# Chunked attention, Fourier mix and MLP: batch 0's first row half unfolded, half sine tables, a second scores buffer, loads in another order

## The chip, the core and the metric

One core of one Trainium2 chip runs the kernel. The metric is the device time of one execution in microseconds, the median of the runs. TensorE is called PE here, VectorE DVE, ScalarE ACT, GpSimd POOL, SyncE SP. PE multiplies into PSUM banks; DVE and ACT read them; POOL works on SBUF only, and the DMA transfers that it starts go out on a queue of its own, as those of SP do on theirs.

## What is computed

```python
# q, k, v: (4, 8, 768, 64); mem_k, mem_v: (4, 8, 8, 64)
for c in range(24):                       # chunks of 32 queries
    k_full = concat(mem_k, k[c_start - 16 : c_end + 8])      # clipped to 0..768
    v_full = concat(mem_v, v[c_start - 16 : c_end + 8])
    out[c] = softmax(q[c] @ k_full.T / 8) @ v_full
x = out as (4, 768, 512)
u = x + real(fft(fft(x, axis=1), axis=2))
un = (u - mean(u)) / sqrt(var(u) + 1e-6)
y = u + relu(un @ w_ch1) @ w_ch2          # w_ch1 (512, 2048), w_ch2 (2048, 512)
```

The real part of the two transforms needs cosine and sine tables over the 768 rows (cosS, sinS) and over the 512 columns (cosD, sinD).

## The kernel before

The four batches go through the same three stages: attention, Fourier mix, MLP. A small planner (class Plan, lines 37 to 174) orders every step: each step has an engine, a cost, what it waits for, the slots that it takes and gives, and a rank. `order` walks through time, puts on each idle engine the ready step of lowest rank, and the instructions are then emitted in that order; on the chip each engine runs its list strictly. Where PE has no ready step between two given events, the planner emits a filler, a multiplication of zeros (`e_fill`, line 899).

**Attention** (line 941) works on pairs of heads, four pairs per batch, in the order 0, 2, 1, 3; n counts them, so n = 0 to 3 is batch 0 and n = 4 the first of batch 1. Per pair, Q and K are loaded by POOL's queue (L349), V by SP's queue in pieces of 256 bytes a row (L358, L362, L367). PE turns Q and K (L377, tiles trq and trk), ACT copies Q (L395), DVE or ACT copies K into kTb (L420) beside the memory keys (L408). Then, for each of two halves g, PE multiplies scores (L433, tile sc, two banks), ACT takes the exponentials (L441, two instructions of 1.05 us together), PE multiplies the values (L457, tile xa for g = 0 and xo for g = 1), and DVE divides by the sums (L467, L468) into the rows of xsb. The one sc tile serves all pairs and both halves. Q and K stage through three buffers each, V through four (va). Rows 0 to 31 of each va are filled with zeros once by ACT (L331), its edges by POOL or DVE, and POOL puts in the ones at the edges (L322, L324, L327) before that pair's V is loaded. POOL also makes the masks (L301 to L307) that the exponentials use. A copy on POOL from the last V tile of batch 0 (L956, "gate") holds back the loads of batch 1.

**Tables.** DVE works out the angles (L920 to L928), ACT takes the sines (L1027 to L1031) of all 2 x 3 x 193 entries for the rows and 2 x 256 for the columns, DVE makes negated copies (L1035, L1038) and sets the first row (L1040, L1041). ACT then loads the table of the exponential (L1048).

**Fourier mix of batch 0** (`first_fourier`, line 1071). The columns 0 to 127 and 256 to 383 come from the pairs n = 0 and 1, the others from n = 2 and 3. For each row half g (three tiles of 128 rows), DVE adds and subtracts the columns (L599), folds them with their mirror image (L610, two steps), ACT rounds to a 16-bit high part (L651), DVE takes the low part (L655), and PE multiplies both parts with the tables (L688: four sums ps, 12 multiplications each and per half). One extra row is handled apart (L661 to L664 on POOL, L669 and L675 on PE). The second half is folded by L616 and L635. Then ACT and DVE split the sums again (L541, L546, L554), PE multiplies over the columns (L699), DVE adds to x (L705) and takes mean and variance (L713), and PE turns the result (L730) for the MLP.

**MLP.** W1 and W2 are loaded by POOL's queue (L1062, L1067), W1 once the second half's first fold is placed, W2 after pair 6's loads (n = 6). Layer 1 is L775, ReLU L784, layer 2 L793 or, for later batches, L842 with sums of weights (L817). PE works on the MLP of one batch while attention and Fourier mix of the next run. PSUM has two banks under the name acc, two under mlp, and tiles tr, sc (two banks) and xa.

Of the kernel before, what the change touches and what calls it, by code (L numbers as in the profile page):

```python
# [10 lines left out]
FP32 = mybir.dt.float32  # L11
# [10 lines left out]
MEM0 = 32  # L22
# [14 lines left out]
class Plan:  # L37
# [6 lines left out]
    WARM = 18.0  # L44
# [47 lines left out]
    def order(self):  # L92
# [9 lines left out]
        while any(waiting.values()):  # L102
# [5 lines left out]
            for e, ts_ in waiting.items():  # L108
# [49 lines left out]
                else:  # L158
                    if e == "PE" and self.filling and self.filling[0]["at"] is not None \
                            and self.filling[1]["at"] is None:  # L160
                        cost = self.FILL * (2.0 if now < self.WARM else 1.0)
                        idle[e] = now + cost
                        placed.append(dict(engine="PE", cost=cost, emit=self.fill, at=now,
                                           done=now + cost))
                        moved = True
# [12 lines left out]
def kernel(  # L178
# [25 lines left out]
    NK = 193  # L204
    HD = DM // 2
# [11 lines left out]

    bank_of, bank_free = {}, {"acc": [0, 1], "mlp": [0, 1]}

    def bank(tag, shape, dtype, name):  # L220
        i = bank_free[tag].pop(0)
        t = fps.tile(shape, dtype, tag=f"{tag}{i}", bufs=1, name=name)
        bank_of[name].append((t, tag, i)) if name in bank_of else bank_of.update({name: [(t, tag, i)]})
        return t
# [12 lines left out]
    ks = [spool.tile([P, 2, RB * D], BF16, name=f"ks{i}") for i in range(NS)]  # L237
    NV = 4
# [25 lines left out]
    tri = fpool.tile([P, 3, 2, HD], FP32, tag="hT", bufs=1, name="tri")  # L264
    kk, yD, rD = tri[:, 0], tri[:, 1], tri[:, 2]
    yS = fpool.tile([P, 3, 2, NK], FP32, tag="fold", bufs=2, name="yS")
    rS = fpool.tile([P, 3, 2, NK], FP32, tag="fold", bufs=2, name="rS")
    sv = cpool.tile([P, 3], FP32)
    svS = cpool.tile([P, 3], FP32)
    svD = cpool.tile([P, 1], FP32)  # L270
    zero = cpool.tile([P, 1], FP32)
# [10 lines left out]
    odd = wpool.tile([P, 2, 3, NK], FP16)  # L282
    cosD = wpool.tile([P, 2, HD], FP16)
# [10 lines left out]
    def e_iota():  # L294
        nc.gpsimd.iota(kk, pattern=[[1, 2], [2, HD]], base=0, channel_multiplier=0,
# [4 lines left out]
    def e_masks():  # L300
# [6 lines left out]
        nc.gpsimd.memset(mbias[MEM0:MEM0 + NMEM, 1:2], 0.0)  # L307

# [20 lines left out]
    def e_low_rows(i):  # L329
        low = va[i][0:MEM0].rearrange("p h t c -> p (h t c)")  # L330
        nc.scalar.copy(low, zero[0:MEM0].to_broadcast([MEM0, 2 * NT * 66]))  # L331
# [8 lines left out]
    def e_load_qk(n, i):  # L340
        b, pr = seq[n]
        src, dst = ((q, qs), (k, ks))[i]
        if b >= TURNED:
            for hh in range(2):
                nc.gpsimd.dma_start(
                    strided(dst[n % NS], hh * D, [[2 * D, NST], [1, D]]),
                    src[b, 2 * pr + hh].rearrange("(a p) d -> p a d", p=P))
            return
        nc.gpsimd.dma_start(dst[n % NS][0:QP],  # L349
# [30 lines left out]
    def e_flip_q(n):  # L380
        qT_of[n] = qT = apool.tile([P, S], BF16, tag="qT", bufs=2, name="qT")
        nc.sync.dma_start_transpose(qT.rearrange("p (a s) -> p a s", s=P),
                                    qs[n % NS].rearrange("p h c -> p (h c)")[:, 0:S])

    def e_flip_k(n):
        nc.sync.dma_start_transpose(kU[n % NKU][:, KR:KR + S].rearrange("p (a s) -> p a s", s=P),
                                    ks[n % NS].rearrange("p h c -> p (h c)")[:, 0:S])

    def e_turn_q(n):
        tr_of[n] = trq = aps.tile([P, S], BF16, tag="tr", bufs=1, name="trq")  # L390
        turn(trq, qs[n % NS][0:QP], ident_b[0:QP, 0:QP])

    def e_qT(n):
        qT_of[n] = qT = apool.tile([P, S], BF16, tag="qT", bufs=2, name="qT")
        nc.scalar.copy(qT.rearrange("p (a j) -> p a j", j=RB),  # L395
                       tr_of.pop(n).rearrange("p (j a) -> p a j", j=RB))

    def e_turn_k(n):
        if n < HP:
            trk = bank("acc", [P, RB * KP], BF16, "trk")  # L400
        else:
            trk = aps.tile([P, RB * KP], BF16, tag="tr", bufs=1, name="trk")
        tr_of[n, 1] = trk
        turn(trk, ks[n % NS][0:KP], turn_b)

    def e_mkT(n):
        b, pr = seq[n]
        (nc.scalar.copy if n == HP else nc.vector.tensor_copy)(  # L408
# [17 lines left out]
    def e_scores(n, g):  # L426
        qT, kT = qT_of[n], kTb[n % NKT]
        sc_of[n, g] = sc = aps.tile([P, 2, 8, 64], FP32, tag="sc", bufs=1, name="sc")
# [50 lines left out]
    mid32 = cpool.tile([P, NST, 1], FP32)  # L479
# [63 lines left out]
    def e_rest(b, par, ab):  # L543
# [4 lines left out]
        let_go(ps)  # L548
# [44 lines left out]
    def g_zy(par, g):  # L593
        if g == 0:
            if par == 0:
                both = fpool.tile([P, 2, NST, P], FP32, tag="dn", bufs=1, name="zy0")
                zy_of[0, 0], zy_of[0, 1] = both[:, 0], both[:, 1]
# [4 lines left out]
    def g_ff(par, ab, g, last):  # L602
        if (ab, g, last) == (0, 0, 0):
            ff_of[0, par] = fpool.tile([P, 2, NST, P], FP32, tag="fold", bufs=2, name="ff0")
        xb, sl = xs[0][:, 3 * g:3 * g + 3], slice(3 * g, 3 * g + 3)
        zy, ff = zy_of[0, par][:, sl], ff_of[0, par][:, ab, sl]
        plus = ab == par
        if last:
            plus = plus == (par == 0)
        nc.vector.tensor_tensor(ff[:, :, 1:P], (ff if last else zy)[:, :, 1:P],  # L610
                                rev_ap(xb, 2 * P - 1 + HD * last, P - 1, [[DM, 3]]),
                                ALU.add if plus else ALU.subtract)
# [6 lines left out]
    def g_col(par, ab, g):  # L619
        zy = zy_of[0, par]  # L620
        ff = ff_of[0, par][:, ab, 3 * g:3 * g + 3]
        if ab == 0:
            nc.scalar.copy(ff[:, :, 0], zy[:, 3 * g:3 * g + 3, 0])
        elif par == 0:
            nc.scalar.copy(ff[:, :, 0], zero[:, 0:1].to_broadcast([P, 3]))
        elif g == 1:
            nc.scalar.copy(ff[:, :, 0], zy[:, 0:3, 0])
        else:
            xb = xs[0][:, 0:3]
            nc.gpsimd.tensor_tensor(ff[:, :, 0], xb[:, :, P], xb[:, :, HD + P], ALU.subtract)  # L630
# [18 lines left out]
    def g_hi(par, ab, g):  # L649
        sl = slice(3 * g, 3 * g + 3)  # L650
        nc.scalar.copy(g_hl(par, 0)[:, ab, sl], ff_of[0, par][:, ab, sl])  # L651

    def g_lo(par, ab, g):
        sl = slice(3 * g, 3 * g + 3)
        nc.vector.tensor_tensor(g_hl(par, 1)[:, ab, sl], ff_of[0, par][:, ab, sl],  # L655
                                g_hl(par, 0)[:, ab, sl], ALU.subtract)

    def g_mid(g):
# [743 lines left out]
```

## Time and profile before

| | |
|---|---|
| time, median of 3 | 282.46 us (281.37 to 285.58) |
| the profiled execution | 282.55 us, span 280.7 us |
| PE busy | 264.3 us (94%) |
| DVE busy | 193.5 us (69%) |
| ACT busy | 155.2 us (55%) |
| POOL busy | 64.3 us (23%) |
| the chain that ended last | PE 84%, DMA 7%, DVE 4%, SP's queue 3% |

Busy time of PE holds the fillers too, and matmuls are pipelined, so it is not work alone. All times in the views count from the first instruction of the span. A group of matmuls with tile names shows what it multiplies: trq is the turned Q, trk the turned K, sc scores, xa and xo values, ps sums over rows, pm sums over columns, ph and pc the two layers, idle the fillers.

Loads and their landings in the first 70 us, from the trace (issue, then landing):

| load | issue | landing |
|---|---|---|
| Q, K of n = 0 | 1.54, 3.06 | 6.03, 9.75 |
| Q, K of n = 1 | 4.75, 5.40 | 12.02, 13.53 |
| Q, K of n = 2 | 8.00, 8.64 | 15.07, 16.01 |
| Q, K of n = 3 | 16.54, 17.18 | 21.43, 23.64 |
| Q, K of n = 4 | 27.98, 28.60 | 32.17, 33.16 |
| W1, four pieces | 34.05 to 35.71 | 42.41 to 50.51 |
| W2, four pieces | 37.51 to 45.31 | 56.44 to 66.25 |
| Q, K of n = 7 | 48.27, 51.07 | 67.51, 68.75 |

V of n = 0 to 3 is issued from 1.36, 6.47, 15.17 and 18.58 us on.

### The profile page before, as it was taken

Reading aid. Unit: us, or ns where it says so; the run is one execution under the profiler, and the core shown is the slowest. Engines: PE = TensorE matmul, PEld = TensorE weight load, DVE = VectorE, ACT = ScalarE, POOL = GpSimd, SP = SyncE. Lnnn points to the kernel's source line nnn. Section 1 sums busy time; section 2 is a strip of 40 time slices with the busy share of each in tenths; the row PEclk is TensorE's granted clock in tenths of the full one; section 3 lists DMA queues with packets and bytes.
Section 4 is the critical chain, followed back from the end, with each engine's and each line's share of the span. In section 5 each row is a group of like instructions: output and inputs, shape, how many; then the busy total and the mean of one; then the engine's idle time right before and its main releaser. Section 6 shows DMA issues by size and latency. Waiting matters only on the chain.

```text
span 280.7 us, 7981 instructions
## 1 busy us (share of the span) xinstructions
PE 264.3 (94%) x3325; PEld 207.4 (74%) x3325; DVE 193.5 (69%) x424; ACT 155.2 (55%) x262; POOL 64.3 (23%) x127
## 2 busy tenths in 40 slices
PE   0589999999999999998999999999999999999995
PEld 0466698788756579766668766858988888888884
DVE  7968978970218979899688776599869825353444
ACT  6887667579665757734745665525526270605150
POOL 8840853240111038306200230101004100000000
PEclk9999999999999999999999999999999999999999
DMA  6989999999899969999999734497101507103152
GB/s 102 199 143 174 162 206 204 196 198 201 162 190 236 214 103 220 177 142 144 235 191 209 177 74 109 108 207 167 48 37 58 131 21 168 40 37 77 50 103 76
DMA packets 116116, 39.98 MB, mean 142 GB/s; under 512 B 104560, under 2 KB 111472, under 8 KB 116080
## 3 DMA queue, kind: packets, MB, share of 16 engines
q1 hardware_dynamic: 93888, 23.54, 46.9%
q0 software_dynamic: 21472, 15.21, 34.0%
q10 hardware_dynamic: 720, 0.72, 0.7%
q8 instruction: 26, 0.43, 0.7%
q14 instruction: 10, 0.08, 0.1%
HBM read 37.36 MB, written 13.37 MB: 181 GB/s over the span
## 4 chain that ended last, share of the span: by engine, by line
PE 84%; DMA 7%; DVE 4%; SPq 3%; issue 1%; POOL 0%; POOLq 0%
PE ph L775 31%; PE pc L793 15%; PE pc L842 13%; DMA va<-in_v_dram 6%; PE ps L529 6%; PE xa L457 4%; PE pm L699 4%; PE ps L688 3%; PE xo L457 3%; PE sc L433 2%; SPq L358 2%; DMA qs<-in_q_dram 1%; PE trk L377 1%; PE trq L377 1%; DVE xsb L705 1%; PE pm L580 1%
## 5 line engine op out<-in xcount | busy, mean ns | idle before, releaser
L775 PE MATMUL ph<-unT,w_sb 128*128 128x256 f16 x768 | 90.3, 273 | 0.8 <-DVE xsb L800 0.8
L784 ACT ACTIVATE hT<-ph 128x512 f16<-128x512 f32 x96 | 56.9, 598 | 54.3 <-PE pc L842 30.2
L775 PEld LDWEIGHTS <-w_sb 128*128 128x128 f16 x768 | 73.2, 98 | 11.1 <-issue 1.7
L793 PE MATMUL pc<-w_sb,hT 128*128 128x512 f16 x192 | 44.8, 380 | 0.0
L441 ACT ACTIVATE e<-sc,mbias 128x384 f32<-128x384 f32 x64 | 33.6, 576 | 19.0 <-PE sc L433 19.0
L793 PEld LDWEIGHTS <-hT 128*128 128x128 f16 x192 | 17.7, 98 | 19.0 <-issue 0.2
L847 DVE TENSOR_TENSOR xsb<-pc,xsb 128x256 f32<-128x256 f32 x43 | 18.0, 421 | 12.4 <-PE pc L842 10.6
L842 PEld LDWEIGHTS <-hT 128*128 128x128 f16 x240 | 23.3, 98 | 4.2 <-DVE hT L830 1.0
L842 PE MATMUL pc<-w_sb,hT 128*128 128x256 f16 x192 | 24.1, 272 | 0.5 <-DVE hT L830 0.5
L541 ACT CAST up<-ps 128x386 f16<-128x386 f32 x16 | 9.7, 605 | 17.6 <-PE ps L529 17.0
L830 DVE TENSOR_TENSOR S<-hT 128x768 f16<-128x768 f16 (+1 forms) x12 | 5.1, 422 | 18.5 <-ACT hT L784 17.9
L800 DVE SCALAR_TENSOR_TENSOR xsb<-pc,rstd,xsb 128x512 f32<-128x512 f32 x12 | 9.0, 750 | 12.2 <-PE pc L793 12.1
L713 DVE BATCH_NORM_STATS2 st<-xsb 128x6 f32<-128x512 f32 x24 | 16.6, 690 | 0.6
L705 DVE TENSOR_TENSOR xsb<-pm,xsb 128x512 f32<-128x512 f32 x15 | 10.2, 678 | 7.1 <-PE pm L699 6.9
L457 PEld LDWEIGHTS xa<-va,e 128*64 128x64 f32 x384 | 12.5, 137 | 3.2 <-issue 2.0
L457 PE MATMUL xa<-va,e 128*64 128x65 f32 x384 | 14.7, 226 | 0.0
L433 PEld LDWEIGHTS <-kTb 64*128 64x128 bf16 x384 | 7.8, 96 | 9.0 <-issue 8.1
L457 PE MATMUL xo<-va,e 128*64 128x65 f32 x384 | 14.1, 223 | 0.0
L546 DVE TENSOR_TENSOR up<-ps,up 128x386 f16<-128x386 f32 x16 | 9.6, 602 | 6.1 <-ACT up L541 6.1
L395 ACT COPY qT<-trq 128x768 bf16<-128x768 bf16 x12 | 9.5, 793 | 6.4 <-PE trq L377 6.4
L572 POOL DMA_DIRECT2D xr<-x_back x3 | 2.3, 770 | 46.7 <-DMA x_back<-x_rows 46.7
L519 DVE TENSOR_TENSOR lo<-ff,hi 128x768 f16<-128x768 f32 x12 | 11.3, 954 | 2.4 <-ACT hi L514 2.4
(168 smaller groups left out, 455.3 us busy)
## 6 DMA issues: line engine op xcount, KB each, us to landing
va<-in_v_dram SPq DMA_DIRECT2D x32, 220.0 KB
w_sb<-in_moe_w_ch_dram POOLq DMA_DIRECT2D x8, 512.0 KB, 16.9
out_dram<-xsb SPq DMA_DIRECT2D x12, 256.0 KB
qs<-in_q_dram POOLq DMA_DIRECT2D x12, 192.0 KB, 6.5
ks<-in_k_dram POOLq DMA_DIRECT2D x12, 192.0 KB, 7.0
x_rows<-xsb POOLq DMA_DIRECT2D x3, 768.0 KB, 4.6
xr<-x_back POOLq DMA_DIRECT2D x3, 768.0 KB, 5.0
out_rows<-xsb SPq DMA_DIRECT2D x9, 256.0 KB
```

Of the source, the lines that this page charges most:

```text
L433: nc.tensor.matmul(sc[:, hh, t6, :], kT[r0:r0 + 64, t, :], qT[r0:r0 + 64, ts(t, 64)], start=True, stop=True, tile_position=(r0, 0))
L441: nc.scalar.activation(e1[:, :, :, ts(half, 32)], sc[:, :, 0:6, ts(half, 32)], AFT.Exp, bias=mbias[:, half:half + 1], scale=1.0 / math.sqr ...
L457: nc.tensor.matmul(xa[64 * half:64 * half + 64, st, hh, 0:65], e1[:, hh, t6, :], v1[:, hh, 6 * g + t6, 0:65], start=True, stop=True)
L519: nc.vector.tensor_tensor(lo[:, ab].rearrange(fl), ff_of[b, par][:, ab].rearrange(fl), hi[:, ab].rearrange(fl), ALU.subtract)
L529: nc.tensor.matmul(out_[:, sp, :], part[:, ab, sp * 3 + st, c0:c1], tab[:, sp, st, :], start=(st == 0 and i == 0), stop=(st == 2 and i == 1))
L705: nc.vector.tensor_tensor(uv, pm_of[b, kt], uv, ALU.add)
L713: nc.vector.bn_stats(st6, xs[b][:, kt, :])
L775: nc.tensor.matmul(ph[:, k, :], w1_sb[:, dt, ts(HH * k + i, P)], unT_of[b, j][:, dt, :], start=(dt == 0), stop=(dt == NDT - 1))
L784: nc.scalar.activation(hT_of[b, j][:, :, i, :], ph, AFT.Relu, bias=0.0, scale=1.0 if b in EVEN else -1.0)
L793: nc.tensor.matmul(pc_of[b, j, r], hT_of[b, j][:, k, i, ts(r, P)], w2_sb[:, HH * k + i, :], start=(i + k == 0), stop=(i + k == HH))
L842: nc.tensor.matmul(pc_of[key], a[:, i, :], w[:, i, :], start=(i == 0 and new), stop=(i == HH - 1), skip_group_check=not new)
L847: nc.vector.tensor_tensor(u, pc, u, ALU.add)
```

## The change

**First row half of batch 0, unfolded.** Instead of folding columns with their mirror before the multiplication, the forward columns (of n = 0 and 1) and the mirrored ones (of n = 2 and 3) are multiplied apart and summed in PSUM; where the fold subtracted, the mirrored product uses a negated table (neg for sp = 0, odd for sp = 1). The sums ps of par 0 lie in the sc tile, those of par 1 in acc.

```diff
+    def g_back(par):
+        nc.vector.tensor_tensor(ff_of[0, par][:, 0, 0:3, 1:P],
+                                rev_ap(xb, 2 * P - 1, P - 1, [[DM, 3]]),
+                                rev_ap(xb, 2 * P - 1 + HD, P - 1, [[DM, 3]]),
+                                ALU.add if par == 0 else ALU.subtract)
+    def g_rows0(par, ab, back):
...
+        for sp in range(2):
+            tab = ((neg, odd)[sp][:, ab] if back and ab != par else (cosS, sinS)[ab][:, sp])
+            for st in range(3):
+                for i in range(2):
+                    nc.tensor.matmul(ps[:, sp, :], g_hl(par, i)[:, back, st, :], tab[:, st, :],
+                                     start=(not back and sp + st + i == 0), stop=False)
...
+                        take=() if back else ("acc",) if par else ("sc",) if ab == 0 else ())
+                    if (par, ab, back) == (1, 0, 1):
+                        t_e2 = add("POOL", 0.4, g_edge2, [t_e1, t_ra[1, 0]], rank=20.2)
```

Column 0 of the mirrored half is set to zero by POOL (`g_edge0`), and for par 1 it takes the middle column, made by POOL before DVE's `g_w` overwrites its input (`g_edge1`) and put in place between the third and the fourth mirrored product (`g_edge2`). The extra row is now multiplied once, after its halves are added and subtracted on POOL (`g_mid`, five small operations; `g_row`, 12 multiplications, no zeroing multiplication).

**Tables by half.** Angles and sines are worked out for 97 of 193 row entries and 129 of 256 column entries; DVE mirrors the rest with a sign (`e_back_S`, `e_back_D`, four instructions, and six on one column in `e_signs`); POOL writes the last column (`e_tails`), makes neg (`e_negatives0`, two instructions of 579 elements) and takes over nsinD and the row memsets.

```diff
-            nc.scalar.activation(sinS[:, par], rS[:, :, par], AFT.Sin, bias=0.0, scale=scS)
+            nc.scalar.activation(sinS[:, :, :, 0:NH], rS.rearrange(order), AFT.Sin, bias=0.0, scale=scS)
+        nc.vector.tensor_scalar(tab[:, :, :, NH:NK - 1],
+                                strided(tab, NH - 2, [[3 * NK - 1, 2], [NK, 3], [-1, NH - 2]]),
+                                sign[:, 1 - i:2 - i], None, ALU.mult)
+    def e_negatives0(i):
+        nc.gpsimd.tensor_scalar(neg[:, i], (cosS, sinS)[i][:, 0], -1.0, None, ALU.mult)
-        nc.vector.tensor_scalar(nsinD, sinD, -1.0, None, ALU.mult)
+        nc.gpsimd.tensor_scalar(nsinD, sinD, -1.0, None, ALU.mult)
```

**Scores in two places.** The two acc banks become views of one tile, accs. In batch 0 the second half's scores (g = 1) go there, the first half's to sc; the turned K of batch 0 goes to mlp instead of acc.

```diff
+    accs = fps.tile([P, 2, 512], FP32, tag="acc", bufs=1, name="accs")
+        sc_of[n, g] = sc = (accs.rearrange("p h (t q) -> p h t q", q=64) if n < HP and g == 1 else
+                            aps.tile([P, 2, 8, 64], FP32, tag="sc", bufs=1, name="sc"))
```

**Loads and small work.** Pair 3 of batch 0 has a stage of its own (last_qk, in the space of w2t), and its loads are issued right behind pair 2's (rank 10.2). The gate reads the first head of pair 3's last V tile instead of the second. W2 is loaded after pair 7's Q and K instead of after pair 6's. Low rows of va 2 and 3 become memsets on POOL, the memory-key copies of batch 0 (`e_mkT`) move from DVE to POOL. The K copies of n = 5, 6, 7 move from ACT to DVE. The turns of a pair in batch 0 get ranks ahead of the scores of the pair before. The weight sums on DVE (`e_w2t`) are placed behind batch 2's statistics.

```diff
-        t_low[i] = add("ACT", 1.45, lambda i=i: e_low_rows(i), [t_zero, e_],
-                       rank=(0, 1, 2, 3)[i])
+        t_low[i] = add("ACT" if i < 2 else "POOL", 1.45 if i < 2 else 1.7, lambda i=i: e_low_rows(i), [t_zero, e_],
+                       rank=(0, 1, 17.3, 17.4)[i])
+                      rank={0: -4 + i, 1: -1.2 + 0.1 * i, 2: 10 + 0.1 * i, 3: 10.2 + 0.1 * i}.get(n)) for i in range(2)]
-            if b == 1 and i in (1, 2):
+            if b == 1 and i in (1, 3):
```

**Fillers.** They now start with the first one at the head of the program (before: with the first scores) and end when the first half product's input is ready (before: when the first folded one is). Each filler takes any free one of the slots mlp, tr and xa for its own length; the planner counts PE as slow until 6 us instead of 18.

```diff
-    WARM = 18.0
+    WARM = 6.0
+                        tag = next((x for x in ("mlp", "tr", "xa") if self.free[x] > 0), None)
-                        plan.filling = (t_sc[0, 0], add("PE", 0.0, lambda: let_go(fill_of[0]), [lo],
-                                                        give=("mlp",)))
+        plan.filling = (t_fill, add("PE", 0.0, lambda: None, [half[0, 0]]))
```

POOL's list in batch 0, by rank: first loads and edge ones, kTb zeros and memory keys, loads of pairs 2 and 3, pad memset of K, tails, masks (16), edges of va 2 and 3 (17), further pads, edge ones of va 2 and 3 (17.1), low rows (17.3, 17.4), neg (17.5, 17.6), edge zeros (18, 19), column-table rows (19.5), kU zeros (20), then the gate and batch 1's loads, with the edge column and the extra row (20.1 to 20.3) ahead of them where ready.

## The prediction

> **What bounds the kernel now.** I read the page's strip of 40 slices first, because it tells where TensorE (PE) is not full.
>
> ```profile
> PE   0589999999999999998999999999999999999995
> DMA  6989999999899969999999734497101507103152
> ```
>
> PE is full from the fourth slice (21 us) to the last: what is not full is the start. The change works there, so the next view is busy time by stage. Columns: stretch, length, then busy us (instructions) of PE, its weight loads, DVE, ACT, POOL; granted clock, DMA share, GB/s.
>
> ```profile
> 0.00:9.00 9.00, 0.77 (x4) 0.26 (x6) 7.48 (x28) 5.52 (x6) 7.75 (x22) 1.00 0.76 123
> 9.00:22.00 13.00, 10.54 (x239) 8.00 (x239) 10.40 (x29) 11.89 (x20) 7.72 (x24) 1.00 1.05 170
> 22.00:33.20 11.20, 10.70 (x226) 7.42 (x224) 9.80 (x24) 7.27 (x18) 4.45 (x10) 1.00 1.00 160
> 33.20:57.10 23.90, 23.25 (x391) 20.34 (x389) 20.79 (x49) 14.68 (x28) 9.80 (x16) 1.00 1.16 201
> ```
>
> The first multiplication of the MLP (L775) starts at 57.1. Up to there PE is busy 45.26 us and idle 11.84. Part of the busy time is filler (L902, multiplications of zeros), as the same stretches restricted to tile idle show (PE busy first):
>
> ```profile
> 0.00:9.00 9.00, 0.50 (x1) 1.00 0.76 123
> 9.00:22.00 13.00, 2.02 (x6) 1.00 1.05 170
> 22.00:33.20 11.20, 4.59 (x23) 1.00 1.00 160
> ```
>
> With 0.14 after 33.2 that is 7.24 us, so work is 45.26 - 7.24 = 38.0 of the 57.1 us. After 57.1 the waits of PE sum to 0.8 + 0.5 us and a tail of some 3. The end therefore moves by what the start of the MLP moves, if nothing behind it runs dry.
>
> The timeline says why the start is slow (start, length, what, idle before it):
>
> ```profile
> 8.95 0.85 PE L377 MATMUL trq<-ident_b,qs 96*64 96x96 bf16 x16
> 9.79 0.88 PE L377 MATMUL trk<-turn_b,ks 100*64 100x100 bf16 x16
> 16.55 1.05 ACT L441 ACTIVATE e<-sc,mbias 128x384 f32<-128x384 f32 x2 [1.08 <-PE sc L433]
> 17.49 1.50 ACT L331 COPY va<-zero 32x1584 f32<-32x1584 f32 x1
> 18.29 0.52 PE L377 MATMUL trk<-turn_b,ks 100*64 100x100 bf16 x16
> 27.44 0.47 POOL L956 COPY gate<-va 1x1 f32<-1x1 f32 x1 [9.63 <-DMA va<-in_v_dram]
> 33.43 1.17 PE L675 MATMUL ps<-cosS,mid 128*1 128x193 f16 x12
> ```
>
> The eight pairs of exponentials of batch 0 run from 13.74 to 30.52: 16.8 us for 8 x 1.05 = 8.4 of work. One scores buffer makes each wait for scores and the scores wait for it, and two fills of low rows (1.50 each) lie between them on ACT. PE's first turns take 0.85 to 0.88 where later ones take 0.5: it is slow until about 17. The gate line is the last landing of V for pair 3, 27.3. From 33.2 on PE is dense.
>
> **The change, part by part.** I book PE's time up to the MLP, then ask when PE becomes dense.
>
> *Work on PE.* Before, 120 table multiplications (96 on L688, 24 on L675) and one zeroing (0.26). After: the first row half unfolded needs 2 halves x 4 sums x 12 = 96, the second half 48, the one-row product 12: 156. At 1.10 / 12 = 0.092 each the 36 more cost 3.3 us, less 0.26. All are on the bounding engine, so they count in full.
>
> *Slow turns.* Fillers now run from 1 us. Four slow turns take 3.37 us start to start (0.84, 0.88, 0.84, 0.81) against 4 x 0.36 warm, two slow scores 0.43 against 0.28, mps about 0.1 more: 2.2 us that go, to the gain. PE had been busy from 12.06 without a gap when the turn at 17.93 was fast and the scores at 16.00 still slow: 4 to 5.6 us of activity. So with fillers from 1.05 the turn of pair 0 at 6 to 9 us is warm or at worst half slow (1 us of the 2.2). The profile's granted clock stands at 1.00 throughout and doesn't show it; only durations do. The Trainium skill ("TensorE: Matmul & The Clock Gate", Part 1) says some 4 us of sustained activity release the gate, as these rows do, and that an idle window of about 3.4 us closes it again, which speaks against ending the fillers at the first half product. By it a hole that long near 21 us would return up to the 2.2 us. No such hole stands in this trace.
>
> *DVE and ACT.* Halved sine tables: six Sin runs of 0.63 to 0.78 become four, two of about 0.7 and two of half the old length, DVE's angle steps (5.0 us for S, 2.4 for D) halve, four mirror copies (0.3 to 0.6) and six one-column ops (0.06 to 0.17) come. The fold of the first half drops from 14 DVE ops to 8 at 0.5 us: 3 us off DVE after pair 3's values. Low rows of pairs 2 and 3 leave ACT (3.0 us). None of this is on PE; it counts through when PE becomes dense.
>
> *When PE becomes dense.* The first exponential needs masks (POOL), scores, and the table load. K of pair 0 landed at 9.75; turn 0.4, copy 1.25, scores 0.35 give 11.8. But POOL now issues pair 3's two loads (1.28) and runs a pad memset (1.0), the tails (0.5) and two mkT copies (about 0.28 each, as on DVE) before the masks (0.9), which ended at 12.2: about 13.3. So the chain starts 0.4 earlier, no more. Then the pairs follow K's landings: 9.75, 13.53, 16.01, and pair 3, issued at about 10 instead of 16.54, two loads later at 1.0 to 1.5 each: 18.6. Turn, copy 1.25, scores: exponentials of pair 3 from 20.6 to 22.8 (30.52 before). The scores' accumulator then goes to the forward products of the first half, which need pairs 0 and 1 only. From 22.0 PE has forward products (48 x 0.092 = 4.4), values of pairs 2 and 3 (4 x 0.75 = 3.0) and a last scores block (0.28): 7.7 us, to 29.7. Mirrored products need V of pair 3. The DMA share was 0.77 from 14 to 16 us, a hole that pair 3's loads now fill; POOL's list puts pair 2's V behind edge_ones at 16.7 (15.17 before), and 1130 KB at the 150 KB/us of the V queue alone (300 KB per 2 us at 22 to 28) end at 25.2. Values 0.8, norm 0.8, mirror add 0.5, high part 0.5, low part 0.5 with hand-overs: 28.7. That is before 29.7, so PE is dense from 22.0.
>
> Bounds for the 22.0: 19.5 if pair 3's K lands as soon as pair 2's did; 25 if the V queue sets it.
>
> *The sum.* Work to the MLP: 38.0 + 3.3 - 0.3 - 2.2 = 38.8. Not work: to 22.0 PE does turns 3.0, scores 7 x 0.28, values of two pairs 3.0, mps 0.1 = 8.1, so 13.9. Then 0.65 of waits on sums between 50 and 54 us, kept, and 0.3 for the new wait of the last mirrored product on POOL's edge column (two ops of 0.2 to 0.49; bounds 0 and 0.8). MLP starts at 38.8 + 13.9 + 0.65 + 0.3 = 53.65, against 57.1: 3.45 us earlier. The profiled execution took 282.55 (span 280.7 and 1.85 around it): 279.1. The median of the runs shown is 0.1 lower. One gap of 0.8 at 128 us, PE waiting for a bank, may go since W2 is now issued behind pair 7's loads (pair 7's K landed at 68.75, after W2's last at 66.25); half of it taken: 278.7.
>
> *What hides the rest.* W1 must land before the MLP: its last piece landed at 50.51, against 53.65 needed, a cover of 3.1 us, or 4, as POOL reaches the issue at 33.0 instead of 34.05 (gate from 27.8, 0.5; four loads 2.5; edge 0.7; one-row sums 1.5). W2's last moves back by two loads (2.6 us at 1.3) from 66.25 to 68.9; first use was 75.68, now 72.2, cover 3.3. Three K copies of batch 1 go from ACT to DVE: 3 x 1.25 us between 50 and 70, where DVE is busy 9.48 of 10 and then 2.33 of 10; at worst 1 us on a sum. The W2 sums on DVE go behind batch 2's statistics; they feed products after 199 us only. Accumulator banks as views of one tile: nothing, as long as each bank waits for itself alone.
>
> *POOL is the risk.* It was free from 17.81 to 27.44. It gains two low-row fills (1584 elements; kU's 800 take 0.74, so 1.5 each), two negations of 579, nsinD of 512 and eight row memsets (0.15), edges, tails: about 11 us, so the gate moves to 27.8 (27.44). A read-modify op has no row of that size: make_identity's select of 128 took 0.29 against 0.18 for 2 elements, so 0.9 ns per element, 0.7 us for 579. Beside DVE it is dearer:
>
> ```profile
> 2.49 0.18 POOL L322 TENSOR_SCALAR_AFFINE_SELECT va<-va 32x2 f32<-32x2 f32 x1
> 6.08 0.46 POOL L322 TENSOR_SCALAR_AFFINE_SELECT va<-va 32x2 f32<-32x2 f32 x1
> ```
>
> The second ran while DVE did L925, which reads two SBUF tensors: 2.5 times, so 0.7 to 1.8 us each. I take 0.8. The Trainium skill ("SBUF — State Buffer", Who interferes with whom) says such a DVE op locks out a POOL op that reads SBUF until it ends. By it each negation could wait one DVE op, 0.5 us, and the gate would slip 1 to 2 us, inside W1's cover.
>
> **Rivals.**
> - *Attention is quicker than booked, and gaps close* (0.25): K of pair 3 at 17, PE dense at 20.5 (1.5 us), no wait on the edge column (0.3), 0.65 and all of 0.8 gone (1.05 more): 275.8. For it: DMA is the only thing between pairs. Against: masks and eight loads on one POOL queue.
> - *V still sets it* (0.2): POOL's edge_ones are later than 16.7 and PE is dense only from 25: 278.7 + 3 = 281.7. For it: DMA share is near 1 in every stage.
> - *POOL becomes the bound* (0.12), the other side: negations and nsinD cost 4 us each, nearer to the power of 6 elements (1.37, L758) than to the select. Three ops booked at 0.8 then add 9.6 us ahead of the gate; W1, issued at 34.05 to 36.27 before and about 1 us sooner by my list, goes out 8.6 later and lands at 59.1. PE, whose fillers have ended, waits from 53.65: 5.5 us, so 284.2; with pair 4 and 5 of batch 1 as late and their sums on DVE behind them, up to 290. It decides once POOL slips by over 4, and the kernel is slower than before from about 8 (4 and the 3.75 won).
> - That the change doesn't do what it says I see no room for: the instructions are explicit.
>
> **How the numbers follow.** Forecast 0.43 at 278.7, own range 277 to 280.5. From 275 to 284 leaves out the slower half of the POOL case and the tail of the quick one, less than 2 in 10. This kernel's measurement tells about 2% from no change: below 276.8 or above 288.1. Faster: the quick case and a quarter of the forecast's lower side, 0.36. Slower: the slow end of the POOL case and what I overlooked on its side, 0.08. Within: 0.56.
>
> **What would show it.** First turn near 0.4 us; pair 3's exponentials over by 23; no filler after 21; MLP's first multiplication near 53.7; gate near 28; W1's last landing before 53. Wrong if: the gate is beyond 32, V of pair 3 lands after 26.5, or PE shows waits on DMA between 57 and 130.

## The result, and the profile after

The changed kernel takes 298.38 us (median of 4 runs, 298.29 to 298.96); the kernel before took 282.07 beside it. The ratio is 1.056, 95% interval 1.047 to 1.065: slower, by 16 us. The forecast was 278.7, the range 275.0 to 284.0.

TensorE's strip of 40 slices (7.4 us each) on the page of the changed kernel:

```profile
PE   6999976899999999889988999999979999999995
```

There are holes now in the sixth to eighth slice and later in places that were full before. Busy time by stage, in the prediction's columns:

```profile
0.00:9.00 9.00, 6.75 (x34) 3.11 (x36) 7.35 (x35) 5.57 (x6) 7.10 (x21) 1.00 0.74 124
9.00:22.00 13.00, 12.12 (x241) 7.28 (x237) 6.73 (x16) 8.48 (x15) 10.63 (x32) 1.00 1.08 181
22.00:33.20 11.20, 10.95 (x254) 9.34 (x253) 10.48 (x25) 7.00 (x16) 10.79 (x25) 1.00 0.70 144
33.20:57.10 23.90, 18.84 (x248) 16.53 (x246) 15.72 (x33) 10.78 (x22) 12.49 (x22) 1.00 1.13 199
```

The last row is the first surprise: PE is busy 18.84 of 23.9 us where it was busy 23.25. The same stretches for the fillers alone (tile idle) are the second:

```profile
0.00:9.00 9.00, 6.56 (x25) 1.00 0.74 124
9.00:22.00 13.00, 7.09 (x29) 1.00 1.08 181
22.00:33.20 11.20, 1.64 (x5) 1.00 0.70 144
```

That is 15.3 us of fillers against 7.24 before, the last of them near 28 us; the prediction wanted none after 21. The timeline's rows for the first turn, the last exponential of batch 0 and the gate:

```profile
8.81 0.53 PE L409 MATMUL trq<-ident_b,qs 96*64 96x96 bf16 x16
...
26.66 1.05 ACT L473 ACTIVATE e<-accs,mbias 128x384 f32<-128x384 f32 x2
...
30.37 0.18 POOL L1017 COPY gate<-va 1x1 f32<-1x1 f32 x1
```

The turn is quick (0.53 us against 0.85 before, near 0.4 forecast); the exponentials end at 27.7 (30.52 before, 22.8 forecast), and the gate opens 3 us later than before. What PE waited for (engine, first tile and line, releaser, us in total, times, longest):

```profile
PE accs L834 <- ACT hT L843: 2.7, 4, 0.7
PE accs L613 <- DVE xsb L764: 2.6, 3, 1.1
PE accs L758 <- DVE up L578: 2.1, 1, 2.1
PE accs L758 <- DVE xsb L764: 1.4, 3, 0.8
...
PE accs L852 <- ACT hT L843: 0.7, 1, 0.7
```

Nearly every new wait is of one kind: PE, about to write one accumulator bank (tile accs), waits for the engine that reads. The timeline shows which bank. Columns: start, length, instruction, and in brackets the idle time before it:

```profile
61.32 1.91 PE L834 MATMUL accs<-unT,w_sb 128*128 128x256 f16 x16
...
63.27 1.08 ACT L843 ACTIVATE hT<-accs 128x512 f16<-128x512 f32 x2 [0.59 <-PE accs L834]
64.40 1.03 PE L834 MATMUL accs<-unT,w_sb 128*128 128x256 f16 x8 [0.73 <-ACT hT L843]
65.47 0.60 ACT L843 ACTIVATE hT<-accs 128x512 f16<-128x512 f32 x1 [1.12 <-PE accs L834]
```

PE fills both banks (16 multiplications, 61.32 to 63.23). The ReLU of the first bank, which is full after half of them, at about 62.3, starts at 63.27: after the second bank. Then PE, whose next product goes into the first bank, starts at 64.40: after both ReLUs (63.27 + 1.08 = 64.35). The two banks have become one.

From the traces I also split the span of each kernel below in the same way. "Not work" is the idle time of PE above 0.12 us and its fillers up to 57 us; "pauses" the idle time above 0.12 us from there to the last multiplication; "work" what is left up to that multiplication; the tail comes after it.

| kernel | not work to 57 us | pauses after | work | tail | span |
|---|---|---|---|---|---|
| before | 18.9 | 1.3 | 257.3 | 3.2 | 280.7 |
| after | 23.2 | 9.3 | 260.9 | 3.2 | 296.6 |
| before_shared_acc | 20.5 | 12.6 | 259.8 | 3.1 | 296.0 |
| after_split_all | 19.1 | 5.2 | 259.3 | 3.7 | 287.3 |
| split_pool_light | 18.3 | 2.8 | 258.9 | 3.6 | 283.6 |
| split_pool_no_fill | 12.2 | 2.6 | 262.8 | 3.6 | 281.2 |
| before_early_fill_2 | 23.8 | 1.9 | 255.4 | 3.2 | 284.3 |

The kernel of before_early_fill was profiled twice, because its first profiled execution ran at a granted clock of 0.76 throughout; the table has the second.

### The profile page after: what moved, and what is told of

It reads as the page before. It is cut to its first block, busy times and chain, and to the rows that moved or that the text cites. A ratio compares the mean times of both kernels' runs of the same rounds, so it can differ in the third digit from the quotient of the medians.

```text
span 296.6 us, 8130 instructions
## 1 busy us (share of the span) xinstructions
PE 275.5 (93%) x3390; PEld 212.3 (72%) x3390; DVE 194.0 (65%) x418; ACT 147.3 (50%) x252; POOL 75.5 (25%) x154
## 4 chain that ended last, share of the span: by engine, by line
PE 77%; DVE 9%; POOL 8%; ACT 4%; issue 2%; DVEq 0%; POOLq 0%; ACTq 0%
PE ph L834 21%; PE pc L901 10%; PE pc L852 9%; PE accs L561 5%; PE accs L834 5%; PE accs L852 5%; PE accs L758 4%; PE xa L489 3%; PE accs L901 3%; DVE xsb L764 2%; PE xo L489 2%; ACT hT L843 2%; PE sc L465 2%; PE idle L960 2%; PE trq L409 1%
## 5 line engine op out<-in xcount | busy, mean ns | idle before, releaser
L834 PE MATMUL ph<-unT,w_sb 128*128 128x256 f16 x624 | 74.9, 273 | 1.2 <-ACT hT L843 1.2
L843 ACT ACTIVATE hT<-ph 128x512 f16<-128x512 f32 x78 | 46.0, 598 | 49.8 <-PE ph L834 23.5
L852 PEld LDWEIGHTS <-hT 128*128 128x128 f16 x192 | 17.3, 98 | 19.5 <-issue 1.7
L852 PE MATMUL pc<-w_sb,hT 128*128 128x512 f16 x128 | 31.1, 380 | 0.0
L834 PE MATMUL accs<-unT,w_sb 128*128 128x256 f16 x144 | 18.3, 272 | 2.7 <-ACT hT L843 2.7
L573 ACT CAST up<-accs 128x386 f16<-128x386 f32 x14 | 8.2, 599 | 23.0 <-PE accs L561 12.7
L843 ACT ACTIVATE hT<-accs 128x512 f16<-128x512 f32 x18 | 10.5, 597 | 17.8 <-PE accs L834 8.3
L889 DVE TENSOR_TENSOR S<-hT 128x768 f16<-128x768 f16 (+1 forms) x12 | 5.1, 424 | 21.2 <-ACT hT L843 20.6
L578 DVE TENSOR_TENSOR up<-accs,up 128x386 f16<-128x386 f32 x14 | 8.2, 596 | 15.8 <-ACT up L573 10.2
L901 PE MATMUL pc<-w_sb,hT 128*128 128x256 f16 x136 | 18.3, 272 | 0.0
L960 PE MATMUL idle<-dz 128*128 128x384 bf16 x59 | 15.3, 366 | 2.1 <-DVE zero L310 1.0
L852 PE MATMUL accs<-w_sb,hT 128*128 128x512 f16 x64 | 15.3, 379 | 1.1 <-ACT hT L843 0.7
L764 DVE TENSOR_TENSOR xsb<-accs,xsb 128x512 f32<-128x512 f32 x15 | 10.3, 684 | 8.5 <-PE accs L758 8.1
L451 DVE COPY kTb<-trk 128x1056 bf16<-128x1056 bf16 x7 | 8.8, 1254 | 6.8 <-PE trk L409 6.7
```

Of the source, the lines that this page charges most:

```text
L764: nc.vector.tensor_tensor(uv, pm_of[b, kt], uv, ALU.add)
L834: nc.tensor.matmul(ph[:, k, :], w1_sb[:, dt, ts(HH * k + i, P)], unT_of[b, j][:, dt, :], start=(dt == 0), stop=(dt == NDT - 1))
L843: nc.scalar.activation(hT_of[b, j][:, :, i, :], ph, AFT.Relu, bias=0.0, scale=1.0 if b in EVEN else -1.0)
L852: nc.tensor.matmul(pc_of[b, j, r], hT_of[b, j][:, k, i, ts(r, P)], w2_sb[:, HH * k + i, :], start=(i + k == 0), stop=(i + k == HH))
L901: nc.tensor.matmul(pc_of[key], a[:, i, :], w[:, i, :], start=(i == 0 and new), stop=(i == HH - 1), skip_group_check=not new)
L960: nc.tensor.matmul(idle[:, 0:384], dz, strided(dz, 0, [[0, 3], [1, P]]), start=True, stop=True)
```

## The experiments

### The shared tile

**before_shared_acc**: the kernel before, and in `bank()` only this (the turned K of batch 0, which lies in the acc banks there, shares a tile in the same way):

```diff
+    accs_of = {}
...
-        t = fps.tile(shape, dtype, tag=f"{tag}{i}", bufs=1, name=name)
+        if tag == "acc":
+            dims = [[math.prod(shape[j + 1:]), n] for j, n in enumerate(shape)][1:]
+            if dtype not in accs_of:
+                accs_of[dtype] = fps.tile([P, 2, 512 if dtype == FP32 else 1024], dtype, tag="acc",
+                                          bufs=1, name="accs")
+            t = strided(accs_of[dtype][:, i, :], 0, dims)
+        else:
+            t = fps.tile(shape, dtype, tag=f"{tag}{i}", bufs=1, name=name)
```

> The kernel before, with one thing of the change alone: the two accumulator banks are views of one tile instead of two tiles; the order of the instructions stays. Theory A (a tile shared by two banks makes TensorE's first write to one bank wait for the reader of the other): in the changed kernel TensorE's pauses of more than 0.12 us after 45 us sum to 12.9 us against 1.95 us before, so this kernel alone should lose some 7 to 11 us, 289 to 293 us, and its waits should name hidden units (accs) waiting for the ReLU, as in the changed kernel. Theory B (the lost time comes from the longer opening and the 36 added table multiplications): 281 to 284 us, no new waits.

Measured: 298.29 us, ratio to before 1.057 (1.053 to 1.061). In the two traces every engine runs the same instructions in the same order, a few semaphore instructions apart. This one edit costs 15.8 us, more than theory A wanted and about as much as the whole change lost. By the table the span grows by 15.3 us: 11.3 are pauses, 1.6 lie in the opening and 2.5 in work, which I did not follow further. Its waits of PE:

```profile
PE accs L707 <- DVE xsb L713: 2.9, 4, 1.5
PE accs L850 <- DVE xsb L855: 1.8, 3, 0.8
PE accs L801 <- DVE xsb L597: 1.7, 2, 0.8
...
PE accs L801 <- DVE up L554: 1.0, 1, 1.0
```

Each reader of one bank now stands in front of the next writer of the other: sums (L713), residual adds (L855), the halves of a sum (L554).

**after_split_acc** and **after_split_all**: the changed kernel with the two banks as tiles again, at first with batch 0's row sums as they were, then with those in tiles of one bank too:

```diff
-            t = strided(accs[:, i, :], 0, dims)
-        else:
-            t = fps.tile(shape, dtype, tag=f"{tag}{i}", bufs=1, name=name)
+        t = fps.tile(shape, dtype, tag=f"{tag}{i}", bufs=1, name=name)
...
+        if n < HP and g == 1:
+            sc = [bank("acc", [P, 8, 64], FP32, "sc1") for _ in range(2)]
...
-                    g_of["ps"] = aps.tile([P, 2, 8, 64], FP32, tag="sc", bufs=1, name="ps")
+            ps_of[0, par, ab] = bank("acc" if par == 0 else "mlp", [P, 2, NK], FP32, "ps")
```

> The changed kernel with the two accumulator banks as tiles of their own again. The second group of batch 0's scores still goes into these two banks, so its two exponentials of 384 columns become four of 192. Theory A: the waits of hidden units for the other bank's ReLU go, 12.9 us of pauses after 45 us fall to 2 to 5 us (the two sums of the first parity still share one tile): 287 to 291 us. Theory B: 297 to 299 us.

> As the run before, and batch 0's four row sums also go to tiles of one bank each (first parity in the accumulator banks, second parity in the two banks of the MLP, where the kernel before had them). Theory A: the sums' waits for the other bank (0.75 us in front of the one-row multiplications, 2.1 us in front of the first column sum, 4.1 us of ScalarE between the two halves of one sum) go as well: 284 to 288 us, MLP start 1 to 3 us earlier than in the run before. Theory B: no change against the run before.

Measured: 288.42 us (ratio to before 1.022) and 288.31 (1.021, 1.015 to 1.028). The banks give back 10 us. The second repair adds nothing that can be told: the pause of 0.75 us in front of the one-row multiplications went, and the MLP started 1.0 us earlier (53.8), but the time stayed. PE's longest waits in after_split_all after the opening:

```profile
PE ph L836 <- DMA unT<-un: 2.4, 1, 2.4
PE ph L836 <- ACT hT L845: 1.1, 2, 0.7
```

The waits that named accs are gone. Theory A is right for 10 of the 16 us, and 6 remain for the rest of the change. The Trainium skill ("PSUM — Partial Sum Buffer", "PSUM bank collisions raise a hardware error") says that two engines on different banks run clean and that accesses want guarding by bank; so by the page the chip did not ask for these waits. The timeline of after_split_all agrees. PE fills three of the four banks in one run of 24 multiplications (56.35 to 59.14), and ACT reads the first from 57.44 and the second from 58.31, while PE still writes the third:

```profile
56.35 2.79 PE L836 MATMUL ph<-unT,w_sb 128*128 128x256 f16 x24
...
57.44 0.60 ACT L845 ACTIVATE hT<-ph 128x512 f16<-128x512 f32 x1
...
58.31 0.60 ACT L845 ACTIVATE hT<-ph 128x512 f16<-128x512 f32 x1 [0.28 <-PE ph L836]
```

### The opening

**split_all_no_fill**: after_split_all with no filler issued at all.

```diff
     def e_fill(tag="mlp"):
...
+        return
```

> As the run before, and none of the 59 idle multiplications of the opening (15.3 us of TensorE in the changed kernel) is issued. If the idle multiplications stand in the way of real work (they share banks with the turned keys and run 0.20 us apart where 0.17 was planned), the first exponential comes earlier than 15.0 us and the whole 0.5 to 2 us sooner. If they do what they are for, keeping the array's early multiplications short, the turns and scores get longer and the whole is 0 to 3 us later. Neither theory A nor B needs a difference here.

Measured: 288.64 us: no difference that can be told. The first exponential came 0.74 us earlier (14.26), but then PE waited 0.85 us for an exponential of pair 3 and 2.6 for its V, until 29.8:

```profile
PE xa L497 <- DMA va<-in_mem_v_dram: 2.6, 1, 2.6
```

Behind this wait the granted clock falls for a while. The stages (in the prediction's columns) before and after 33.5 us:

```profile
30.00:33.50 3.50, 3.50 (x53) 3.29 (x49) 1.96 (x6) 0.00 (x0) 1.72 (x6) 0.51 0.59 110
33.50:36.00 2.50, 2.50 (x32) 2.50 (x31) 2.50 (x7) 1.31 (x4) 2.27 (x6) 1.00 1.17 200
```

The row products start 0.16 us apart up to 33.4 us and 0.085 apart after it. So a hole in the opening costs twice here: its own length, and slow multiplications behind it. The profiled execution is the slowest of the four (290.19).

**split_v_early** (from after_split_all) and **split_v_early_no_fill** (from split_all_no_fill):

```diff
-        v1, eng = va[i], nc.vector if i < 2 else nc.gpsimd
+        v1, eng = va[i], nc.vector
...
-        e_ = add("DVE" if i < 2 else "POOL", 0.45, lambda i=i: e_edges(i),
-                 rank=(-20, -17.3, 17, 17)[i])
-        t_ones[i] = add("POOL", 0.7, lambda i=i: e_edge_ones(i), [e_], rank=(-3.5, 2, 17.1, 17.1)[i])
+        e_ = add("DVE", 0.45, lambda i=i: e_edges(i), rank=(-20, -17.3, -8, -7)[i])
+        t_ones[i] = add("POOL", 0.7, lambda i=i: e_edge_ones(i), [e_], rank=(-3.5, 2, 10.5, 10.6)[i])
```

> Base: the run after_split_all (288.3 us). V's edge columns of pairs 2 and 3 are set by DVE (idle at that time) and POOL's ones stand right behind pair 3's loads, so SP can issue V of pair 2 from about 12.5 instead of 15.5 us. Theory C (the opening stayed as long as before because V's arrival sets it): the first row product comes 1 to 2 us sooner than 30.1, the whole at 286 to 287.5 us. Theory D (the fixed order of the opening sets it: in after_split_all the 59 idle multiplications run 0.20 us apart instead of the 0.17 that the program counts with, and what stands behind them on TensorE comes late whatever lands early): no change, 288 to 289 us.

> Base: split_all_no_fill (288.6 us), where TensorE waited 3.5 us for V of pair 3 until 29.8 us; with V early as in split_v_early. Theory C: that wait falls to under 1.5 us, row products start near 30 instead of 32.2, the whole at 286 to 287.5 us. If V is slow because the DMA engines are full (their share is 0.9 and more from 7 to 22 us) and not because it is issued late: the wait stays above 2.5 us and the whole at 288 to 289 us.

Measured: 286.10 and 284.99 us, 2.2 and 3.6 less than their bases. The intervals of the first two touch (ratio to before 1.012, 1.006 to 1.018, against 1.015 to 1.028), those of the others do not (1.005 to 1.011 against 1.016 to 1.026). V of pair 2 was issued at 12.05 instead of 15.51 (12.22 without fillers). Without fillers theory C holds for the opening: the wait for V shrank from 2.6 us to 0.14 and the first row product came at 30.1 instead of 32.2; the time ended 1 us below its range. Its record of the clock has no such fall, so part of the 3.6 us is the slow stretch that its base had. With fillers the number fits theory C and the reason doesn't: the first row product came later, at 31.4, since POOL's ones now delay the masks (first exponential 16.2). What shrank there are the pauses after 57 us, from 5.2 to 3.1.

**split_pool_light**: the negations and table rows on DVE.

```diff
-        nc.gpsimd.tensor_scalar(neg[:, i], (cosS, sinS)[i][:, 0], -1.0, None, ALU.mult)
+        nc.vector.tensor_scalar(neg[:, i], (cosS, sinS)[i][:, 0], -1.0, None, ALU.mult)
...
-        nc.gpsimd.tensor_scalar(nsinD, sinD, -1.0, None, ALU.mult)
+        nc.vector.tensor_scalar(nsinD, sinD, -1.0, None, ALU.mult)
...
```

> Base: after_split_all. The negations (neg, nsinD) and the table rows go back to DVE (there three tensor operations of 0.3 to 0.4 us and eight memsets of 0.16), which takes some 6.5 us off POOL ahead of the gate at 30.6 us. Theory E (POOL's longer list delays batch 1's loads): the gate falls to 27 to 28.5 us, K of pair 4 lands 2 to 5 us sooner than 39.6, the whole gains 1 to 3 us: 285 to 287. If POOL is covered, as the prediction said, the gate moves and the time does not: 288 us within 0.7.

Measured: 285.49 us, 2.8 less (ratio to before 1.012, 1.008 to 1.015; the interval just touches that of its base). The gate went from 30.6 to 25.3 us and K of pair 4 landed at 32.4 instead of 39.6, both further than expected. The two pauses at the edge column (0.8 together) went, and the pauses after 57 us fell from 5.2 to 2.8. So the number fits theory E, and POOL was not covered. That the earlier loads of batch 1 made the gain is not shown: most of it is the pauses near 130 us. The negations in the changed kernel, and the same two on DVE here (line, engine, form, ns):

```profile
L1122 POOL TENSOR_SCALAR neg<-cosS x1: 1698/1698/1698, 22.6 to 22.6; 128x579 f16<-128x579 f16 x1
L1122 POOL TENSOR_SCALAR neg<-sinS x1: 1665/1665/1665, 24.3 to 24.3; 128x579 f16<-128x579 f16 x1
```

```profile
L1124 DVE TENSOR_SCALAR neg<-cosS x1: 309/309/309, 14.2 to 14.2; 128x579 f16<-128x579 f16 x1
L1124 DVE TENSOR_SCALAR neg<-sinS x1: 1106/1106/1106, 17.2 to 17.2; 128x579 f16<-128x579 f16 x1
```

**split_pool_light_fill20**: the planner counts a filler at what it takes, `FILL = 0.20` for 0.17.

> Base: split_pool_light (285.5 us); the program counts an idle multiplication at 0.20 us, as measured, instead of 0.17, so it puts fewer of them ahead of real work. Theory D (the slip of the fixed order comes from them): first row product 0.7 to 1.5 us earlier than 30.3, whole 284 to 285. If the order slips for other reasons (loads, copies): 285 to 286.5.

Measured: 285.72 us, first row product at 30.55: nothing. Eight fillers fewer did not straighten the order, so theory D is not borne out in this form.

**split_values_first**: from split_pool_light.

```diff
-                     rank=len(plan.tasks) + (50 if (n, g) == (2, 1) else 25) if first else None,
+                     rank=len(plan.tasks) + (0 if n < 2 else 50 if (n, g) == (2, 1) else 25) if first else None,
```

> Base: split_pool_light (285.5 us). The value multiplications of pairs 0 and 1 get the rank of their place in the program instead of 25 ranks later, so they go ahead of the turns and scores of the pairs behind. In split_pool_light the first row product waits, at 30.3 us, for a chain from pair 1's values (23.1 to 24.7) over divisions, sum, high and low part. If that chain sets the opening, the first product comes at 27.5 to 29 us and the whole at 284 to 285. If TensorE has work enough until then, or the exponentials of pairs 2 and 3 come later by what pair 1 gains: 285.5 to 287.

Measured: 289.94 us, 4.4 more. The first row product came at 34.2, the last exponential ended at 30.95 instead of 28.41. Values ahead of scores make the scores late: the second outcome, and dearer than I thought.

**before_early_fill**: the kernel before with the change's filler code alone, its three slots and WARM of 6 us included (86 fillers in place of 29).

```diff
-    WARM = 18.0
+    WARM = 6.0
...
-                        plan.filling = (t_sc[0, 0], add("PE", 0.0, lambda: let_go(fill_of[0]), [lo],
-                                                        give=("mlp",)))
+                        plan.filling = (t_fill, add("PE", 0.0, lambda: None, [lo]))
```

> The kernel before with one part of the change alone: its idle multiplications start at the head of the program and take any free one of three slots, to the first folded product. It tests the term 'slow turns: 2.2 us that go' by itself. If the term is right and what is saved reaches the end: turns of pair 0 take 0.5 to 0.55 us instead of 0.85, the first exponential is 13 us instead of 13.7, and the whole gains 1 to 2.2 us: 280.3 to 281.5. If the opening waits for loads anyway (Q and K land at 9.75 and 13.5, V later), the saving is refilled by waiting: 282 to 283 us.

Measured: 285.47 to 289.69 us, ratio to before 1.016 (1.005 to 1.026). The same kernel, profiled again:

> The kernel of before_early_fill once more, for a profile that can be read: 285 to 288 us. If the early idle multiplications stand in the way, first exponential and first row product come later than in the kernel before (13.74 and 35.0 us) by the 3 to 5 us that the whole is longer. If instead the order behind the opening changed, the opening is the same or shorter and pauses or busy time after 57 us are longer.

Measured: 286.06 us, ratio 1.011 (1.007 to 1.016). Tile idle in it:

```profile
0.00:9.00 9.00, 6.14 (x24) 1.00 0.76 129
9.00:22.00 13.00, 8.12 (x39) 1.00 1.13 196
```

The fillers do what they are for: turns take 0.53 us from the first on, and work falls by 1.9 us, near the 2.2 of the prediction. But not-work grows by 4.9. The first exponential starts at 14.22 (13.74 before), the last one ends at 33.34 (30.52): each engine runs its list in the planner's order, and ten fillers (15.42 to 17.44 us) stand in front of the second half's scores of pair 0, which went at 16.0 before.

**split_pool_no_fill** and **split_v_pool_no_fill**: the repairs together.

> Base: split_pool_light (285.5 us) without its 59 idle multiplications. In split_all_no_fill leaving them out changed nothing (288.6 against 288.3), because V of pair 3 was late then. If V still is (it waits there for POOL's edge columns): a wait of 2 to 3 us for V and 285.5 to 287 us. If POOL's shorter list brings V forward too: 283.5 to 285 us.

> Base: split_v_early_no_fill (285.0 us), with POOL's negations and table rows on DVE as in split_pool_light. If the two repairs add up (V early was worth 3.6 us without idle multiplications, POOL's list 2.8): 282 to 283 us, the same as the kernel before (282.4). If both pay for the same wait: 284.5 to 285.5 us.

Measured: 284.24 us (ratio to before 1.006, 1.003 to 1.009) and 285.96 (1.011, 1.008 to 1.014). The profiled execution of the first is the fastest of its ten (282.97). In it not-work to 57 us is 6.8 us less than before and the first row product comes at 28.2; yet the last multiplication ends at 277.6 as before, since work has grown by 5.5: some 3.1 by the 36 more multiplications (84 of them take 7.24 us in a row, 0.086 each). The rest fits turns, scores and values that stay slow up to 20 us, but I did not add it up. The two repairs do not add up: V early costs the opening masks that come late (first exponential 16.2 instead of 14.3). No version I ran beats the kernel before.

### The edits outside the opening

**split_late_undone** and **before_late_edits**: the three edits taken out of after_split_all, and put alone into the kernel before.

```diff
-    KDVE, QDVE = (5, 6, 7), ()
+    KDVE, QDVE = (), ()
...
-                              rank=MLPS + len(plan.tasks), behind=t_stats[2, 5]))
+                              rank=MLPS + len(plan.tasks)))
...
-            if b == 1 and i in (1, 3):
+            if b == 1 and i in (1, 2):
```

> Base: after_split_all. The three edits outside the opening are undone: W2 is loaded behind pair 6 again, the K copies of pairs 5 to 7 go back to ScalarE, the sums of W2 have no place behind batch 2's statistics. Theory F (these edits make the pauses after 100 us, 5.2 us against 1.3 in the kernel before): pauses fall to 1 to 2.5 us and the whole to 284 to 286 us. If the pauses come from the shifted order alone: 287.5 to 289 us.

> The kernel before with the change's three edits outside the opening alone (W2 behind pair 7, K copies of pairs 5 to 7 on DVE, sums of W2 behind batch 2's statistics). In the changed kernel with split banks they were worth 4.6 us (288.3 against 292.9 without them), by a wait of 7.7 us for a turn by DMA that they avoid; the kernel before has no such wait, so here they can win at most its 1.3 us of pauses after 100 us. Expected: 281.5 to 284 us; a gain of 3 us or more would say that they help by themselves.

Measured: 292.92 us, 4.6 more than after_split_all, and 282.46, the same as before (ratio 1.000, 0.996 to 1.003). The first lies above both ranges. Theory F falls: these edits do not make the late pauses. Without them the one wait for a turn by DMA grows:

```profile
PE ph L836 <- DMA unT<-un: 7.7, 1, 7.7
```

Pauses account for 3.2 of the 4.6 us. Work grows by 1.3, and behind the wait the granted clock falls (its mean is 0.987 to 0.988 in all four runs):

```profile
134.40:141.30 6.90, 4.56 (x22) 3.21 (x23) 2.12 (x4) 1.19 (x2) 1.68 (x2) 0.51 0.85 150
```

In after_split_all these turns stand on SP's queue behind the V loads of later pairs; the first of four is issued at 127.1, the last ends at 132.4, and PE resumes at 132.5. In the kernel before the same turns were issued from 123.7 on, in split_pool_light from 119.2. So I read the late pauses as a product of the order that the planner made out of the new opening, which the late edits soften; no run isolates it.

before_late_edits shows one thing more. Its MLP starts at 54.0, 3.1 us sooner than the 57.1 of the kernel before, and its time is the same.

## Why the prediction was wrong, step by step

- **"Accumulator banks as views of one tile: nothing, as long as each bank waits for itself alone."** This is the step that failed. The condition does not hold: a bank waits for the other bank's reader. It is worth 10.1 us in the changed kernel (298.4 against 288.3) and 15.8 in the kernel before. I wrote the condition down and gave it no price and no rival, though the diff showed the shared tile. Even without it the 288.3 us would lie above the range of 275 to 284, by the steps that follow.
- **"PE is dense from 22.0" (bounds 19.5 to 25).** The first row product came at 29.9. The first exponential was at 15.0 (booked 13.3), the exponentials of pair 3 from 24.9 to 27.7 (booked 20.6 to 22.8), although K of pair 3 landed at 19.30, near the 18.6 booked. Not-work up to the MLP was booked at 13.9 + 0.65 + 0.3 = 14.85; in after_split_all it is 19.1, as much as before (18.9). That is 4.3 us. Fillers, turns and scores stand in one fixed order, and early delays are handed on: values of pair 0 began at 20.1, 3 us after its exponentials. No single one of them sets the opening: the first row product came at 32.2 without fillers (split_all_no_fill), at 31.4 with V early, at 30.1 with both, and at 28.2 without fillers and with POOL relieved (split_pool_no_fill). The V sum in this step is also 1 us off: 16.7 + 1130/150 gives 24.2, not 25.2; the miss does not rest on it.
- **"If nothing behind it runs dry."** The MLP of after_split_all starts at 53.8, as forecast (53.65), and the kernel is still 6 us slower than before. The start of the MLP was no ruler, as before_late_edits shows too: the values of pairs 4 and 5 and the scores of pair 5 were done when the MLP of the kernel before started, and here they had moved behind it. Pauses after 57 us went from 1.3 to 5.2 where I had booked a drop of 0.4: another 4.3 us.
- **Slow turns.** The size was right (1.9 us measured for 2.2, in before_early_fill_2), but it was a gain only on paper: the fillers that brought it cost 4.9 us of not-work. The hole that this step warned of did come once, in split_all_no_fill, with the clock at 0.51 behind it. The 1.00 that I read for the cold opening was no reading; the last section says why.
- **Added multiplications.** Right: 3.1 for 3.3. Work as a whole rose by 2.0 us in after_split_all where 0.8 was booked.
- **POOL.** Negations took 1.70 and 1.67 us and nsinD 1.49, within my bounds (0.7 to 1.8), not at the 0.8 that I took. The gate came at 30.4 instead of 27.8 and W1's last piece landed at 53.5. "Inside W1's cover" was wrong: 2.8 us come back when POOL is relieved, though not by W1, for which PE does not wait. The POOL rival named the right engine at too high a price (4 us an operation).
- **"V still sets it"** showed only with the fillers gone: 2.6 us of waiting, from 27.2 to 29.8.
- **The signs of being wrong.** Two of them did not come up (gate at 30.4, not beyond 32; no wait on DMA between 57 and 130 us in the changed kernel), so they would not have pointed at the shared tile.

Set against the forecast's span (278.7 - 1.85 = 276.85), the 296.6 measured is 19.7 longer: 9.3 shared tile (296.6 - 287.3), 4.3 opening, 4.3 late pauses, 1.2 work and 0.5 tail; together 19.6.

Three things have no measurement: fillers only ahead of the first real multiplication, the kernel before without fillers, and pair 3's stage of its own in the kernel before. Whether the earlier loads gain anything by themselves stays open. So does why relief on POOL shortens pauses some 100 us later; V loads and turns stand in another order on SP's queue then, but I did not isolate it.

## What to carry to other kernels

Give each PSUM bank that is written and read in turn a tile of its own, and where a diff merges two, price the case that each writer waits for the other bank's reader. In a program that runs a fixed list per engine, an idle multiplication is not free: count idle time, fillers and the slow work of the opening together, and judge an opening by that sum, not by when the next stage starts. A step that is moved out of a short idle stretch changes the order of everything planned behind it, so expect pauses far away (here at 130 us) and leave room for them in the range.

## What the runs showed of the hardware

The same negation on DVE took 0.31 us once and 1.11 the other time. The timeline of split_pool_light shows what lay beside the second:

```profile
17.17 0.95 POOL L946 MEMSET ks<- 4x1024 bf16 x1
17.18 1.11 DVE L1124 TENSOR_SCALAR neg<-sinS 128x579 f16<-128x579 f16 x1
```

POOL's memset began 0.01 us earlier and ended at 18.12; DVE ended at 18.29, 0.17 us after it. The Trainium skill ("SBUF — State Buffer", Who interferes with whom) says that DVE's two-port fast modes and POOL share a port pair, that whoever issues first holds it for the whole instruction and that the other blocks. These rows agree in kind: DVE took 0.80 us longer beside a memset of 0.95. A wait for all of it with 0.31 of work behind would have ended at 18.43, and one pair is all that I looked at. On POOL the same negation of 579 16-bit elements a row costs 1.70 us, more than five times DVE's 0.31.

The rows show a granted clock of 1.00 through the opening, whether a turn takes 0.85 us (kernel before) or 0.53 (changed kernel). That is no reading: the trace's record of the clock begins at 16.4 us in the kernel before and at 4.9 in the changed one, and the views give 1.00 where there is no record. From there on the turns are quick in both (0.53 at 17.93 and at 8.81). Where a record exists, durations follow it. In split_pool_light_fill20 PE pauses from 4.9 to 6.8 us, the record stands at 0.5 from 7.5 to 11.0, and the turn at 9.00 takes 0.85.
